# Attention before two MoE layers on one core: zero-padded q in place of stacked operands, the gate moved into the normaliser, the order of the steps rewritten

## The chip, the cores and the metric

One core of one Trainium2 chip. The time is that of one execution on the device in microseconds (us); less is better. The kernel before takes 941.54 us as the median of 3 runs (940.49 to 942.72).

## What is computed

In short form:

```python
scores = scale * np.matmul(q, k.transpose(0, 1, 3, 2))      # B, H, S, D = 4, 8, 576, 64
a = softmax(causal(scores)); local = np.matmul(a, v)
q_p = np.where(q > 0, q, np.exp(q) - 1.0) + 1.0
mem_out = (q_p @ M_prev) / (q_p @ z_prev + 1e-6)
x = g * mem_out + (1 - g) * local                            # g = sigmoid(beta), one per head
h = x @ w_in; solu = h * softmax(h)                          # 2304 tokens, 512 -> 1024
x = (layernorm(solu) * g_ln) @ w_out                         # -> 512
out = (sigmoid(x @ w_gate) * (x @ w_val)) @ w_out2           # 512 -> 1536 -> 512
```

Weights of the MoE layers arrive as 64-bit floats and are turned into 32-bit ones on the chip.

## The kernel before

The attention works on 16 pairs of heads (4 batches by 4 pairs). The two heads of a pair lie on partitions 0 to 63 and 64 to 127. For a pair n the steps are: q and k are loaded and transposed on PE (`tq_p`, `tk_p`), scaled and split into a high part in the fast matmul format and a rest (`tq_h`, `tq_l` at L270 and L274; `tk_h`, `tk_l`); the scores are computed in five blocks (`s0_p` to `s4_p`, L366 to L389: block i is 128 queries against 128(i+1) keys for both heads, block 4 the last 64 queries of both heads against all 576 keys); DVE adds the mask, copies the block to SBUF and takes its maximum (`s_m`, L409), ACT takes the exponential and the row sum (`s_e`, L417), POOL multiplies by the reciprocal of the sum (`n_p`, L426); PE transposes the blocks (`g`, `t`, `tt`, `tc`), DVE or ACT copies them out of PSUM, and PE multiplies by v (`x_a`, L496) on top of the memory part (`x_m`, L481).

A score needs three products: high q with high k, low q with high k, high q with the rest of k. From pair 1 on, the kernel before does the first two as one matmul: Z (L286) holds the high and the low part of one head of q stacked on 128 partitions, W (L313) the high part of k twice. Z, W and Zm (high q with the other head's half zeroed, for the third product) are filled by ten transfers from SBUF to SBUF for each pair (`tq_d`, `tk_d`, L293, L296, L316). Block 4 uses qb, a block-diagonal copy of the last queries that POOL writes (`tq_b`, L279). In pair 0 the three products are matmuls over 64 partitions (L385).

The gate g is applied to the memory matrix by POOL (`sm`, L363). One sixteenth of w_in is converted for each pair (`cv_d` load; `cv_a`, `cv_b` on DVE, L105, L106, L114, L115; `cv_r` on ACT, L109; `cv_p`, four operations on POOL, L529, L530, L135, L138).

The table ORDER sets the order of the work by hand: a loop walks it once for each value of `it` from -3 to 18, and an entry such as `tq_p:1` issues that step for pair it+1. Each engine runs its own share of that order strictly one after another. PSUM is divided among three tags: `s`, two buffers of two banks each, which the transposes of q, k and E and the five score blocks take in turn; `t`, two buffers, for the transposed blocks; `x`, two buffers. A step that takes a buffer waits until the buffer's user before last has been copied out.

After the attention come the first MoE layer (`Moe1`) and the second (`Moe2`), whose code the change does not touch.

Of the kernel before, what the change touches and what calls it, by code (L numbers as in the profile page):

```python
# [8 lines left out]
F32 = mybir.dt.float32  # L9
# [11 lines left out]
ORDER = """  # L21
s4_e:-1 s1_p:0 tf_c:-1 cv_a:-1 ph_e:0 s1_m:0 tq_p:1 g1_p:-1 a14:-2 a12:-2 tq_b:0 n2_p:-1 a13:-2 g1_c:-1 tq_h:1
a10:-2 a01:-2 a00:-2 n3_p:-1 s0_p:0 tq_l:1 n4_r:-1 g0_p:-1 t1_p:-1 s2_p:0 cv_r:-1 s1_e:0 g0_c:-1 ph_m:0 n4_p:-1
t1_c:-1 s0_m:0 tk_d:1 cv_b:-1 lv:-1 x1_c:-2 tt_p:-1 x0_c:-2 tt_c:-1 ph_g:0 t3_p:-1 lk:2 s2_m:0 t3_c:-1 s3_p:0
s0_e:0 s4_p:0 lq:2 sm:-1 cv_p:-1 t2_p:-1 tc_p:-1 x0_m:-1 s2_e:0 ph_r:0 tq_d:1 t2_c:-1 cv_d:0 ph_s:0 s3_m:0 lz:2
n01_r:0 s3_e:0 tk_p:2 x1_m:-1 tc_c:-1 s4_m:0 tk_h:2 n23_r:0 a11:-1 t0_p:-1 tf_p:0 t0_c:-1 n1_p:0 n0_p:0 tk_l:2
""".split()
# [20 lines left out]
def kernel(  # L48
# [16 lines left out]
    nc = tc.nc  # L65
# [42 lines left out]
    def f64_r(ex):  # L108
        nc.scalar.activation(ex, ex, AF.Relu, bias=ebias, scale=16.0)  # L109

    def f64_b(raw, ex, mt):
        top = raw[:, :, 1]
        low = raw.rearrange("p n t -> p (n t)").bitcast(U16).rearrange("p (n u) -> p n u", u=4)[:, :, 1]
        nc.vector.scalar_tensor_tensor(ex, top, -0x80000000, ex, ALU.bitwise_and, ALU.bitwise_or)  # L114
        nc.vector.scalar_tensor_tensor(f32(mt), low, 2.0**-16, mt, ALU.mult, ALU.add)  # L115

# [27 lines left out]
    class Attention:  # L144
        def __init__(self, sb, ps, xe):
# [152 lines left out]

# [7 lines left out]
        def tk_l(self, n, r):  # L306
            r["kl"] = self.sb.tile([P, S], F32R, tag="kl", name=f"kl{n}", bufs=2)
            nc.vector.tensor_sub(r["kl"], r["kps"], f32(r["kh"]))

        def tk_d(self, n, r):  # L310
            if n == 0:
                return
            W = self.sb.tile([P, 2, S0], F32R, tag="W", name=f"W{n}", bufs=2)  # L313
            for hh in range(2):
                for d in range(2):
                    nc.sync.dma_start(  # L316
                        f32(W[64 * d : 64 * d + 64, hh]), f32(r["kh"][64 * hh : 64 * hh + 64, :S0])
                    )
            r["W"] = W

# [39 lines left out]

        def sm(self, n, r):
            hp = pairs[n][1]
            nc.gpsimd.tensor_scalar(r["mt"], r["mt"], self.gp[:, hp : hp + 1], 1.0, ALU.mult, ALU.mult)  # L363


        def s_p(self, n, r, i):  # L366
            ps = r["s", i] = self.psum([P, 2, 512], f"sc{n}_{i}")
            kh, kl = r["kh"], r["kl"]
            if i == NB:
                qb = self.qb[n % 2]  # L370
                for j in range(2):
                    x = ps[:, j, : S // 2]
                    sl = slice(j * S // 2, (j + 1) * S // 2)
                    nc.tensor.matmul(x, qb[:, 0], kh[:, sl], start=True, stop=False)
                    nc.tensor.matmul(x, qb[:, 1], kh[:, sl], start=False, stop=False)
                    nc.tensor.matmul(x, qb[:, 0], kl[:, sl], start=False, stop=True)
                return
            w = P * (i + 1)
            for hh in range(2):
                sl = slice(64 * hh, 64 * hh + 64)  # L380
                x = ps[:, hh, :w]
                if n == 0:
                    F = r["F"]
                    for j, (c, kk) in enumerate(((1, kh), (0, kh), (0, kl))):
                        nc.tensor.matmul(x, F[sl, c, w - P : w], kk[sl, :w], start=j == 0, stop=j == 2)  # L385
# [495 lines left out]
```

## Time and profile before

| | |
|---|---|
| median of 3 runs | 941.54 us |
| the profiled execution, its own time | 940.15 us |
| its span in the profile | 938.4 us |
| attention, to the first matmul of `h` | 263.83 us |
| the two MoE layers | 674.57 us |
| granted TensorE clock, mean | 0.993 |

The profile is of one execution. PE is the matmul engine, PEld its weight load, DVE, ACT and POOL the vector, scalar and GpSimd engines, SP the engine that issues the transfers. A row of the timeline gives a start, a duration and, in brackets, how long the engine stood idle before it and which instruction's end released it. Durations of neighbouring rows overlap a little, since an engine starts the next instruction before the last one's result is written; where the text counts what an instruction adds to a queue it takes the distance from start to start. The end of a matmul is modelled: a matmul's 0.4 us include the way of its last column through the array, while the next one may start 0.12 to 0.23 us after it.

### The profile page before, as it was taken

The numbers are of one execution on the slowest core, as the hardware profiler recorded it, in microseconds if no ns is written. First come the engines' busy times: TensorE is split into PE (matmuls) and PEld (weight loads), VectorE is DVE, ScalarE is ACT, GpSimd is POOL, SyncE is SP. The second block draws the span as 40 slices with busy tenths as digits, with TensorE's granted clock in tenths as the row PEclk, the third lists the DMA queues.
The fourth block names the chain that finished last, engine by engine and source line by source line (L and its number), as shares of the span: only waits on it lengthen the run. The fifth ranks groups of instructions, "written<-read, shape, count | busy, mean of one in ns | idle before, by whom it ended". The sixth has DMA issues, their size and how long they took to land.

```text
span 938.4 us, 13939 instructions
## 1 busy us (share of the span) xinstructions
PE 881.5 (94%) x5104; PEld 732.5 (78%) x5104; DVE 572.7 (61%) x1268; ACT 415.0 (44%) x877; POOL 315.3 (34%) x420
## 2 busy tenths in 40 slices
PE   5888888888899999999999999999999999999998
PEld 3656665656677899999989888888888888888887
DVE  5788888888769564584764237637338845333324
ACT  3677777777757655565545233212112212111111
POOL 3777777778956321120510014112005203000000
PEclk9899999999999999999999999999999999999999
DMA  6776777777422110030220003203002200000112
GB/s 137 162 178 155 169 174 163 170 163 165 111 64 72 46 46 24 23 90 1 70 67 1 1 1 113 67 1 90 1 1 91 90 0 1 1 1 1 45 45 112
DMA packets 88291, 68.28 MB, mean 73 GB/s; under 512 B 65056, under 2 KB 65056, under 8 KB 88224
## 3 DMA queue, kind: packets, MB, share of 16 engines
q1 hardware_dynamic: 88224, 67.41, 27.9%
q8 instruction: 40, 0.66, 0.3%
q14 instruction: 27, 0.22, 0.1%
HBM read 43.00 MB, written 4.72 MB: 51 GB/s over the span
## 4 chain that ended last, share of the span: by engine, by line
PE 65%; DVE 5%; POOL 3%; issue 1%; ACT 1%; DMA 0%; POOLq 0%; ACTq 0%; DVEq 0%
PE gv L759 32%; PE po L778 16%; PE po L677 9%; PE h L626 7%; PE pl L665 1%; POOL p L426 1%; DVE exwo L106 0%; DVE exwo L115 0%; DVE exwo L105 0%; DMA rawg<-in_moe_w_gate_dram 0%; DVE exwo L114 0%; DVE lnT L132 0%; POOL rd L646 0%; PE x L496 0%; DVE hm L633 0%
## 5 line engine op out<-in xcount | busy, mean ns | idle before, releaser
L765 DVE TENSOR_TENSOR sg<-sg,gv 128x512 f32<-128x512 f32 (+1 forms) x60 | 38.0, 633 | 175.9 <-ACT sg L764 175.9
L764 ACT ACTIVATE sg<-gv 128x512 f32<-128x512 f32 (+1 forms) x60 | 33.1, 552 | 233.7 <-PE gv L759 233.7
L759 PE MATMUL gv<-xx,gh 128*128 128x512 f32 (+1 forms) x480 | 136.2, 368 | 0.2 <-ACT xx L131 0.2
L759 PE MATMUL gv<-xx,vh 128*128 128x512 f32 (+1 forms) x480 | 136.1, 368 | 0.0
L677 PE MATMUL po<-lnT,woh 128*128 128x256 f32 x576 | 105.5, 285 | 1.0 <-ACT woh L604 0.7
L759 PEld LDWEIGHTS gv<-xx,gh 128*128 128x128 f32 x480 | 87.3, 188 | 16.1 <-issue 0.4
L759 PEld LDWEIGHTS gv<-xx,vh 128*128 128x128 f32 x480 | 87.1, 189 | 15.0
L426 POOL TENSOR_SCALAR p<-p,rs 128x256 f32<-128x256 f32 (+2 forms) x144 | 83.9, 598 | 32.0 <-DVE rs L422 26.1
L677 PEld LDWEIGHTS po<-lnT,woh 128*128 128x128 f32 x576 | 91.0, 193 | 2.5 <-ACT woh L604 0.9
L759 PE MATMUL gv<-xx,gl 128*128 128x512 f32 (+1 forms) x240 | 88.3, 368 | 0.0
L759 PE MATMUL gv<-xx,vl 128*128 128x512 f32 (+1 forms) x240 | 88.3, 368 | 0.0
L417 ACT ACTIVATE p<-p,nm 128x256 f32<-128x256 f32 (+2 forms) x144 | 83.0, 581 | 8.1 <-DVE nm L409 8.0
L626 PE MATMUL h<-wih,xs 128*128 128x512 f32 x288 | 81.8, 397 | 2.6 <-DVE e L639 2.5
L778 PE MATMUL po<-oh,GVxs 128*128 128x512 f32 x216 | 84.1, 389 | 0.0
L778 PE MATMUL po<-ol,GVxs 128*128 128x512 f32 x216 | 84.1, 389 | 0.0
L778 PE MATMUL po<-oh,GVe 128*128 128x512 f32 x216 | 84.0, 389 | 0.0
L677 PE MATMUL po<-lnT,wol 128*128 128x256 f32 x288 | 81.9, 286 | 1.1 <-POOL wol L138 1.1
L785 DVE TENSOR_TENSOR X<-X,po 128x512 f32<-128x512 f32 x90 | 61.4, 684 | 23.2 <-PE po L778 23.2
L135 POOL TENSOR_SCALAR gh<-exg 128x512 fp32r<-128x512 f32 x12 | 9.8, 826 | 173.2 <-PE gv L759 142.1
L626 PEld LDWEIGHTS h<-wih,xs 128*128 128x128 f32 x288 | 53.5, 190 | 13.9 <-ACT e L648 2.9
L409 DVE CUSTOM_DVE_ANT_0 p<-sc,mask 128x256 f32<-128x256 f32 (+3 forms) x128 | 56.1, 474 | 2.1 <-PE sc L389 2.1
L677 PEld LDWEIGHTS po<-lnT,wol 128*128 128x128 f32 x288 | 55.4, 193 | 1.3 <-POOL wol L138 1.3
(363 smaller groups left out, 1855.5 us busy)
## 6 DMA issues: line engine op xcount, KB each, us to landing
W<-kh SPq DMA_DIRECT2D x60, 128.0 KB, 3.1
Z<-F SPq DMA_DIRECT2D x60, 128.0 KB, 2.4
rawg<-in_moe_w_gate_dram SPq DMA_DIRECT2D x12, 512.0 KB, 3.9
rawv<-in_moe_w_val_dram SPq DMA_DIRECT2D x12, 512.0 KB, 3.9
rawo<-in_moe_w_out_dram SPq DMA_DIRECT2D x12, 512.0 KB, 3.4
out_dram<-X SPq DMA_DIRECT2D x18, 256.0 KB, 2.0
kt<-in_k_dram SPq DMA_DIRECT2D x32, 128.0 KB, 2.6
qt<-in_q_dram SPq DMA_DIRECT2D x32, 128.0 KB, 2.7
```

Of the source, the lines that this page charges most:

```text
L135: nc.gpsimd.tensor_scalar(hi, src, scale, 1.0, ALU.mult, ALU.mult)
L409: nc.vector.tensor_tensor_reduce(p, x, m, -1.0, 3.0e38, ALU.add, ALU.min, nm)
L417: nc.scalar.activation(p, p, AF.Exp, bias=nm, scale=-1.0, accum_out=r["sum"][:, c : c + 1])
L426: nc.gpsimd.tensor_scalar(p, p, r["rs"][:, c : c + 1], 1.0, ALU.mult, ALU.mult)
L626: nc.tensor.matmul(ph[:, j * 512 : j * 512 + 512], xs[:, s, c], w[:, j * 512 : j * 512 + 512], start=(c == 0 and s == 0 and w is hi), stop ...
L665: nc.tensor.transpose(pl[:, c], ln[:, f * P : f * P + P], ident)
L677: nc.tensor.matmul(po[:, :GW], w[:, m * P : m * P + P], L[:, x, c], start=(c == 0 and n == 0), stop=(c == NF1 - 1 and n == 2),)
L759: nc.tensor.matmul(ps[:, j, :w], wt[:, c, fs], xx[:, x, c], start=(c == 0 and n == 0), stop=(c == NC - 1 and n == 2),)
L764: nc.scalar.activation(sg[:, :w], ps[:, 0, :w], AF.Sigmoid)
L765: nc.vector.tensor_mul(sg[:, :w], sg[:, :w], ps[:, 1, :w])
L778: nc.tensor.matmul(po, GV[x][:, f, sl], wt[:, f], start=(f == 0 and n == 0), stop=(f == NCH - 1 and n == 2),)
L785: nc.vector.tensor_add(acc[:, t], acc[:, t], po)
```

## The change

- `tq_h` and `tq_l` write straight from PSUM into q2, one tile for each parity of the pair, zeroed once at the start: 128 partitions by (high, low) by 1152 columns. Head 0's 576 columns have zeros on partitions 64 to 127, head 1's have zeros on partitions 0 to 63, and the last 64 queries of the two heads lie side by side, so that block 4 is a slice of it. That takes three instructions on ACT and three on DVE (64 partitions by 576, 512 and 64 columns) in place of one each over 128 by 576.
- All five score blocks are three matmuls over 128 partitions for each half, in all pairs, against kh and kl. Z, W, Zm, F and qb go, with `tq_d`, `tk_d`, `tq_b`.
- `sm` goes. The row normaliser takes the gate: the 128x10 addition on DVE becomes a scalar_tensor_tensor with a second tile g10 (1 + exp(-beta) five times over, built once in `gates`).
- Of the four POOL operations of the w_in conversion one stays (`cv_p`); the scaling goes to ACT (in `cv_r`), the high part to ACT (`cv_h`), the rest to DVE (`cv_l`), and the scaling by 2^-20 also enters `cv_b`'s constant. The raw tile gets two buffers.
- ORDER is new.

```diff
 ORDER = """
-s4_e:-1 s1_p:0 tf_c:-1 cv_a:-1 ph_e:0 s1_m:0 tq_p:1 g1_p:-1 a14:-2 a12:-2 tq_b:0 n2_p:-1 a13:-2 g1_c:-1 tq_h:1
...
+n23_r:-1 s1_e:0 s4_m:0 tt_c:-1 tc_c:-1 s3_m:0 lk:1 cv_r:-1 n3_p:-1 s0_e:0 s4_e:0 x1_c:-2 a00:-2 g1_p:-1 tf_p:0
...
+CVL = "v"
...
-    def f64_b(raw, ex, mt):
+    def f64_b(raw, ex, mt, scale=None):
...
+            nc.vector.scalar_tensor_tensor(f32(mt), low, 2.0**-16 * scale, f32(mt), ALU.mult, ALU.add)
...
-            self.F1 = sb.tile([P, 2, S], F32R, tag="tmp", name="F1")
...
-                qb = sb.tile([P, 2, P], F32R, tag=f"qb{n}", name=f"qb{n}")
-                nc.gpsimd.memset(f32(qb), 0.0)
-                self.qb.append(qb)
-                Zm = xe.tile([P, 2, S0], F32R, tag="e", name=f"Zm{n}")
+
+                q2 = sb.tile([P, 2, 2 * S], F32R, tag=f"q2{n}", name=f"q2{n}")
                 for hh in range(2):
-                    nc.gpsimd.memset(f32(Zm[64 - 64 * hh : 128 - 64 * hh, hh]), 0.0)
-                self.Zm.append(Zm)
+                    nc.gpsimd.memset(f32(q2[64 - 64 * hh : 128 - 64 * hh, :, hh * S : hh * S + S]), 0.0)
+                self.q2.append(q2)
...
+        def q_parts(self, n, r):
+
+            for hh, src, dst in ((0, 0, 0), (1, 0, S + TL), (1, S0, S)):
+                sl, w = slice(64 * hh, 64 * hh + 64), S if hh == 0 else S0 if src == 0 else TL
+                yield r["qps"][sl, src : src + w], *(self.q2[n % 2][sl, c, dst : dst + w] for c in range(2))
+
         def tq_h(self, n, r):
...
+            for x, hi, _ in self.q_parts(n, r):
+                nc.scalar.mul(hi, x, QS)
 
         def tq_l(self, n, r):
...
+            for x, hi, lo in self.q_parts(n, r):
+                nc.vector.scalar_tensor_tensor(lo, x, QS, f32(hi), ALU.mult, ALU.subtract)
...
-        def tq_b(self, n, r):
...
-        def tq_d(self, n, r):
...
-        def tk_d(self, n, r):
...
-            nc.vector.tensor_scalar_add(nr, nr, 1e-6)
+            nc.vector.scalar_tensor_tensor(nr, nr, 1e-6, self.g10[:, pairs[n][1]], ALU.add, ALU.mult)
...
-        def sm(self, n, r):
-            hp = pairs[n][1]
-            nc.gpsimd.tensor_scalar(r["mt"], r["mt"], self.gp[:, hp : hp + 1], 1.0, ALU.mult, ALU.mult)
...
+            q2, kh, kl = self.q2[n % 2], r["kh"], r["kl"]
+            for j in range(2):
+                if i == NB:
+
+                    ks, x = slice(j * S // 2, (j + 1) * S // 2), ps[:, j, : S // 2]
+                    qs = [q2[:, c, S0 : S0 + P] for c in range(2)]
                 else:
...
+                    w = P * (i + 1)
+                    ks, x = slice(0, w), ps[:, j, :w]
+                    q0 = w - P + j * (S + TL)
+                    qs = [q2[:, c, q0 : q0 + P] for c in range(2)]
+                for m, (c, kk) in enumerate(((0, kh), (1, kh), (0, kl))):
+                    nc.tensor.matmul(x, qs[c], kk[:, ks], start=m == 0, stop=m == 2)
...
-            r["raw"] = self.sb.tile([P, 256, 2], I32, tag="raw", name=f"raw{n}")
+            r["raw"] = self.sb.tile([P, 256, 2], I32, tag="raw", name=f"raw{n}", bufs=2)
...
         def cv_r(self, n, r):
             f64_r(r["ex"][:, 0])
+            nc.scalar.mul(f32(r["ex"][:, 1]), r["ex"][:, 1], 2.0**-20)
...
-            nc.gpsimd.tensor_scalar(m, m, 2.0**-20, 1.0, ALU.mult, ALU.mult)
-            nc.gpsimd.tensor_mul(m, m, e)
-            hi, lo = (x[:, 256 * j : 256 * j + 256] for x in wi[c])
-            pool_hi(hi, m)
-            pool_lo(lo, m, hi)
+            m, _, _ = self.cv_parts(n, r)
+            nc.gpsimd.tensor_mul(m, m, f32(r["ex"][:, 0]))
+
+        def cv_h(self, n, r):
+            m, hi, _ = self.cv_parts(n, r)
+            nc.scalar.copy(hi, m)
+
+        def cv_l(self, n, r):
+            m, hi, lo = self.cv_parts(n, r)
+            (nc.vector if CVL == "v" else nc.gpsimd).tensor_sub(lo, m, f32(hi))
```

PE around `trf`, the transpose of E that the first `trq` after it waits for through its copy. Names carry the pair: trf5 is pair 5's, sc6_1 block 1 of pair 6's scores, t5a1 and t5b0 transposed blocks. Before:

```order
L258 MATMUL trf5_1388<-ident_58,E5_1195 128x128 x5
L388 MATMUL sc6_1_1402<-W6_1272,Z6_1344 128x256
L389 MATMUL sc6_1_1402<-kl6_1182,Zm0_120 128x256
L388 MATMUL sc6_1_1402<-W6_1272,Z6_1344 128x256
L389 MATMUL sc6_1_1402<-kl6_1182,Zm0_120 128x256
L258 MATMUL trq7_1419<-ident_58,qt1_94 128x128 x5
```

and now (x4_0 is a product with v of pair 4; between the two pieces stand the rest of t5b2 and two rows of t5b0):

```order
L352 MATMUL sc6_3_1432<-kl6_1356,q20_117 128x512
L459 MATMUL x4_0_1345<-A4_1271,vt1_106 64x256 x2
L398 MATMUL t5a1_1472<-ident_58,p5_1_1193 128x128 x2
L265 MATMUL trf6_1475<-ident_58,E6_1298 128x128 x5
L411 MATMUL t5b3_1481<-ident_58,p5_3_1241 128x128 x2
L352 MATMUL sc6_2_1492<-kh6_1343,q20_117 128x384 x2
L352 MATMUL sc6_2_1492<-kl6_1356,q20_117 128x384
L352 MATMUL sc6_2_1492<-kh6_1343,q20_117 128x384 x2
L352 MATMUL sc6_2_1492<-kl6_1356,q20_117 128x384
...
L411 MATMUL t5b0_1504<-ident_58,p5_2_1329 128x128
L411 MATMUL t5b0_1504<-ident_58,p5_3_1241 128x128
L265 MATMUL trq7_1518<-ident_58,qt1_93 128x128 x5
```

Before, one score block of four matmuls stands between `trf` and the next `trq`; now a transposed block, score block 2 with six matmuls, and three more transposed blocks (t5b3, t5b2, t5b0) stand there. Block 2 now follows `trf`, and block 3 stands before it.

DVE around the low part of q (F before, q20 now; kl is k's low part, nr the normaliser, nm a block's maximum). Before:

```order
L409 ISA nm_1417 128x1
L128 COPY A5_1438<-t5a1_1425 128x2x128
L274 SCALAR_TENSOR_TENSOR F7_1440<-trq7_1419,F7_1440 128x576
L421 SCALAR_TENSOR_TENSOR rs5_1258<-sum5_1257,o9_273 128x1
L422 RECIPROCAL rs5_1258<-rs5_1258 128x1
L330 TENSOR_SCALAR E6_1412<-E6_1412 128x640
L331 SCALAR_TENSOR_TENSOR E6_1412<-qt0_93,E6_1412 128x640
```

and now:

```order
L306 TENSOR_SCALAR E6_1298<-E6_1298 128x640
L307 SCALAR_TENSOR_TENSOR E6_1298<-qt0_92,E6_1298 128x640
L284 SCALAR_TENSOR_TENSOR q20_117<-trq6_1305,q20_117 64x576
L284 SCALAR_TENSOR_TENSOR q20_117<-trq6_1305,q20_117 64x512
L284 SCALAR_TENSOR_TENSOR q20_117<-trq6_1305,q20_117 64x64
L295 TENSOR_TENSOR kl6_1356<-trk6_1337,kh6_1343 128x576
L321 TENSOR_REDUCE nr6_1378<-G6_1358 128x10
L322 SCALAR_TENSOR_TENSOR nr6_1378<-nr6_1378,g10_174 128x10
L323 RECIPROCAL nr6_1378<-nr6_1378 128x10
L372 ISA p6_1_1406,nm_1407<-sc6_1_1392,mask_94 128x256
```

Before, the low part of q stands behind a copy of a transposed block (A5) and ahead of the E and block 0 of pair 6; now E stands ahead of it, and it is followed by k's low part and the normaliser before the first score block (pair 6, block 1) is read.

## Rows read from the trace of the kernel before

**Rows 1.** The page, part 1: busy time of each engine, share, instructions.
```profile
PE 881.5 (94%) x5104; PEld 732.5 (78%) x5104; DVE 572.7 (61%) x1268; ACT 415.0 (44%) x877; POOL 315.3 (34%) x420
```

**Rows 2.** Windows view, four stretches: start:end us, length, busy us per engine, PEclk, DMA, GB/s.
```profile
0.00:25.33 25.33, 13.55 (x60) 9.49 (x60) 14.44 (x58) 10.57 (x27) 9.99 (x25) 0.98 0.67 140
25.33:239.82 214.49, 179.97 (x1344) 133.02 (x1344) 181.87 (x529) 159.34 (x418) 163.22 (x252) 0.99 0.73 167
239.82:263.83 24.01, 21.98 (x175) 14.83 (x174) 13.80 (x47) 15.99 (x41) 19.45 (x31) 1.00 0.24 70
263.83:938.40 674.57, 665.98 (x3530) 575.20 (x3528) 362.57 (x635) 229.12 (x393) 122.67 (x114) 0.99 0.13 40
```

**Rows 3.** Timeline of PE, one pair: start us, us, line, out<-in, [idle before <-releaser].
```profile
118.82 0.28 PE L388 MATMUL sc<-W,Z 128*128 128x256 f32 x1
118.94 0.28 PE L389 MATMUL sc<-kl,Zm 128*128 128x256 f32 x1
120.17 0.77 PE L258 MATMUL trq<-ident,qt 128*128 128x128 f32 x5 [0.95 <-ACT f L128]
...
123.68 0.28 PE L388 MATMUL sc<-W,Z 128*128 128x128 f32 x1
123.79 0.27 PE L389 MATMUL sc<-kl,Zm 128*128 128x128 f32 x1
...
125.15 0.33 PE L388 MATMUL sc<-W,Z 128*128 128x384 f32 x1
125.32 0.34 PE L389 MATMUL sc<-kl,Zm 128*128 128x384 f32 x1
...
126.62 0.39 PE L388 MATMUL sc<-W,Z 128*128 128x512 f32 x1
126.85 0.40 PE L389 MATMUL sc<-kl,Zm 128*128 128x512 f32 x1
128.08 0.40 PE L374 MATMUL sc<-kh,qb 128*128 128x288 f32 x1 [0.84 <-DVE nm L409]
...
129.62 0.65 PE L481 MATMUL x<-f,mt 128*64 128x256 f32 x4
131.01 0.77 PE L258 MATMUL trk<-ident,kt 128*128 128x128 f32 x5 [0.74 <-DVE nm L409]
```

**Rows 4.** Timeline of ACT in the same pair.
```profile
126.61 0.38 ACT L128 COPY Bt<-t6b 128x256 f32<-128x256 f32 x1
...
133.62 0.58 ACT L128 COPY Bt<-t6b 128x512 f32<-128x512 f32 x1 [1.18 <-PE t6b L448]
...
134.88 0.63 ACT L128 COPY f<-trf 128x576 f32<-128x576 f32 x1
...
136.49 0.65 ACT L270 ACTIVATE F<-trq 128x576 fp32r<-128x576 f32 x1 [0.34 <-DMA W<-kh]
```

**Rows 5.** Timeline of DVE in the same pair.
```profile
121.78 0.76 DVE L274 SCALAR_TENSOR_TENSOR F<-trq,F 128x576 fp32r<-128x576 f32 x1 [0.17 <-ACT F L270]
...
130.25 0.09 DVE L409 DVE_READ_ACCUMULATOR2_ANT nm<- 128x1 f32 x1
...
130.87 0.09 DVE L409 DVE_READ_ACCUMULATOR2_ANT nm<- 128x1 f32 x1
...
135.63 0.29 DVE L105 TENSOR_SCALAR ex<-raw 128x256 int32<-128x256 int32 x1 [2.23 <-DMA raw<-in_moe_w_in_dram]
...
137.17 0.76 DVE L274 SCALAR_TENSOR_TENSOR F<-trq,F 128x576 fp32r<-128x576 f32 x1
```

**Rows 6.** Source views of L114, L115, L346: count, duration ns min/median/max.
```profile
L114 DVE SCALAR_TENSOR_TENSOR ex<-raw,ex x16: 422/1586/1598, 31.5 to 254.3; 128x256 int32<-128x256 int32 x16
...
L115 DVE SCALAR_TENSOR_TENSOR ex<-raw,ex x16: 409/412/1779, 33.0 to 254.9; 128x256 f32<-128x256 uint16 x16
...
L346 DVE TENSOR_SCALAR nr<-nr x16: 173/741/748, 21.3 to 248.5; 128x10 f32<-128x10 f32 x16
```

**Rows 7.** The page, part 6: the transfers into W.
```profile
W<-kh SPq DMA_DIRECT2D x60, 128.0 KB, 3.1
```

More of the change, by code (lines that the diff above doesn't have):

```diff
@@ L21 @@
 ORDER = """
-s4_e:-1 s1_p:0 tf_c:-1 cv_a:-1 ph_e:0 s1_m:0 tq_p:1 g1_p:-1 a14:-2 a12:-2 tq_b:0 n2_p:-1 a13:-2 g1_c:-1 tq_h:1
[L23 to L26, printed above, removed]
+n23_r:-1 s1_e:0 s4_m:0 tt_c:-1 tc_c:-1 s3_m:0 lk:1 cv_r:-1 n3_p:-1 s0_e:0 s4_e:0 x1_c:-2 a00:-2 g1_p:-1 tf_p:0
+t3_p:-1 g1_c:-1 tf_c:0 n2_p:-1 t3_c:-1 x0_c:-2 s2_p:0 t2_p:-1 t0_p:-1 cv_b:-1 ph_e:1 t2_c:-1 n4_r:0 n01_r:0 tq_p:1
+cv_p:-1 n1_p:0 lz:1 t0_c:-1 t1_p:-1 g0_p:-1 cv_h:-1 tq_h:1 s2_m:0 t1_c:-1 ph_m:1 tk_p:1 tk_h:1 x0_m:-1 x1_m:-1
+a13:-1 tq_l:1 tk_l:1 ph_g:1 n0_p:0 n4_p:0 cv_d:1 lv:0 a12:-1 a11:-1 a14:-1 a10:-1 ph_r:1 lq:2 ph_s:1 s3_e:0 s2_e:0
+a01:-1 s1_p:1 s0_p:1 s1_m:1 tt_p:0 s0_m:1 g0_c:-1 tc_p:0 s4_p:1 cv_l:-1 s3_p:1 cv_a:0
 """.split()
 COPY = dict(tf="s", tc="v", tt="s", kh="s", x0="v", x1="s", g0="s", g1="v", t0="s", t1="s", t2="s", t3="s")
+CVL = "v"
 def f32(ap):
@@ L114, in f64_b @@
         nc.vector.scalar_tensor_tensor(ex, top, -0x80000000, ex, ALU.bitwise_and, ALU.bitwise_or)
-        nc.vector.scalar_tensor_tensor(f32(mt), low, 2.0**-16, mt, ALU.mult, ALU.add)
+        if scale is None:
+            nc.vector.scalar_tensor_tensor(f32(mt), low, 2.0**-16, mt, ALU.mult, ALU.add)
+        else:
+            nc.vector.scalar_tensor_tensor(f32(mt), low, 2.0**-16 * scale, f32(mt), ALU.mult, ALU.add)
     def load_f64(raw, ex, mt, src):
@@ L170, in __init__ @@
                 nc.vector.memset(t[64:128, tail], 0.0)
-            self.p4, self.qb, self.Zm = [], [], []
+            self.p4, self.q2 = [], []
             for n in range(2):
@@ L194, in gates @@
             sb, bt = self.sb, self.bt
-            nc.vector.tensor_scalar_add(bt, bt, 1.0)
+            nc.vector.tensor_scalar(bt, bt, 1.0, 1e30, ALU.add, ALU.min)
+            bth = bt.rearrange("p (a h) -> p a h", h=2)
+            self.g10 = sb.tile([P, HP, 10], F32, tag="g10", name="g10")
+            for c in range(NB + 1):
+                nc.vector.tensor_copy(self.g10[:, :, 2 * c : 2 * c + 2], bth)
             nc.vector.reciprocal(bt, bt)
-            bth = bt.rearrange("p (a h) -> p a h", h=2)
             self.gp = sb.tile([P, HP], F32, tag="gp", name="gp")
@@ L308, in tk_l @@
             nc.vector.tensor_sub(r["kl"], r["kps"], f32(r["kh"]))
-        def tk_d(self, n, r):
[L311 to L319, printed above, removed]
         def ph_e(self, n, r):
@@ L359, in tf_c @@
             copy("tf", r["f"], r["fps"])
-        def sm(self, n, r):
-            hp = pairs[n][1]
-            nc.gpsimd.tensor_scalar(r["mt"], r["mt"], self.gp[:, hp : hp + 1], 1.0, ALU.mult, ALU.mult)
         def s_p(self, n, r, i):
             ps = r["s", i] = self.psum([P, 2, 512], f"sc{n}_{i}")
[L368 to L385, printed above, removed]
-                else:
-                    Z, W = r["Z"], r["W"]
-                    nc.tensor.matmul(x, Z[:, hh, w - P : w], W[:, hh, :w], start=True, stop=False)
-                    nc.tensor.matmul(x, self.Zm[n % 2][:, hh, w - P : w], kl[:, :w], start=False, stop=True)
+            q2, kh, kl = self.q2[n % 2], r["kh"], r["kl"]
[3 more added lines that the diff above has]
+                    qs = [q2[:, c, S0 : S0 + P] for c in range(2)]
+                else:
+                    w = P * (i + 1)
[4 more added lines that the diff above has]
+                    nc.tensor.matmul(x, qs[c], kk[:, ks], start=m == 0, stop=m == 2)
         def parts(self, r, i):
@@ L521, in cv_r, with cv_parts @@
             f64_r(r["ex"][:, 0])
+            nc.scalar.mul(f32(r["ex"][:, 1]), r["ex"][:, 1], 2.0**-20)
         def cv_b(self, n, r):
-            f64_b(r["raw"], r["ex"][:, 0], r["ex"][:, 1])
+            f64_b(r["raw"], r["ex"][:, 0], r["ex"][:, 1], 2.0**-20)
+        def cv_parts(self, n, r):
+            c, j = divmod(n, 4)
+            return f32(r["ex"][:, 1]), *(x[:, 256 * j : 256 * j + 256] for x in wi[c])
         def cv_p(self, n, r):
-            c, j = divmod(n, 4)
-            m, e = f32(r["ex"][:, 1]), f32(r["ex"][:, 0])
-            nc.gpsimd.tensor_scalar(m, m, 2.0**-20, 1.0, ALU.mult, ALU.mult)
-            nc.gpsimd.tensor_mul(m, m, e)
-            hi, lo = (x[:, 256 * j : 256 * j + 256] for x in wi[c])
-            pool_hi(hi, m)
-            pool_lo(lo, m, hi)
+            m, _, _ = self.cv_parts(n, r)
[6 more added lines that the diff above has]
+            (nc.vector if CVL == "v" else nc.gpsimd).tensor_sub(lo, m, f32(hi))
         def run(self):
```

26 lines of the change are left out of this document (removed).

## The prediction

> **What bounds the kernel now.** The page's first part puts PE at 94% of the span [rows 1], which reads as if only PE's work counted. The windows view says where that is false. I cut the span at the first score block of pair 1, that of pair 15 and the first matmul of `h` [rows 2]. The last stretch, 674.57 us of MoE with PE busy for 665.98, is left alone by the change. In the middle stretch, 214.49 us for 14 pairs or 15.32 us each, nobody is full: per pair PE is busy for 12.86, DVE 12.99, ACT 11.38, POOL 11.66.
>
> So a ring of waits sets the pace there, and PE's timeline shows it. In one pair PE stands idle three times, for 0.95, 0.84 and 0.74 us, before `trq`, score block 4 and `trk` [rows 3]. All three wait for one of the two `s` buffers in PSUM. Counted from start to start they are longer, since a matmul's modelled end lies behind the moment at which the next may start: the last of 512 columns starts at 126.85 and takes 0.23, so block 4, at 128.08, came 1.00 late; `trq` came 1.11 late (118.94 + 0.12 to 120.17); for `trk` I take its 0.74 and the same 0.17 more, 0.91. That is 3.0 us of waits and 12.3 us of PE's own work in a pair.
>
> The ring itself: DVE runs through from the low part of q (121.78) to the maximum of block 3 (130.95), 9.2 us; that frees `trk` at 131.01; PE goes on to a transposed block that ACT copies at 133.62; ACT's copy of f (134.88 to 135.51) frees the next `trq`, which is `trq` at 120.17 a pair later; ACT's high part follows at 136.49 and DVE's low part at 137.17 [rows 3 to 5]. 121.78 to 137.17 is 15.39 us: the ring is closed, and it passes through DVE, PE and ACT.
>
> **The change part by part.** *Transfers out.* Ten of 128 KB a pair, 60 into W alone [rows 7]. Their only mark on the ring is 0.34 us before ACT's high part [rows 4]. DVE's wait of 2.23 us for raw [rows 5] ends in time: the low part of q starts at 137.17, and ACT's high part, which it needs, ends at 136.49 + 0.65 = 137.14 [rows 4]. So neither raw's second buffer nor the freed queue is worth anything by itself. If the ring stayed, 0.34 us a pair, 5 us in all, is what the transfers could give.
>
> *Scores.* Each head's block gets a third matmul: 8 more a pair. Start to start one costs 0.11 us at 128 columns, 0.12 at 256, 0.17 at 384 and 0.23 at 512 [rows 3], so 2 x 0.63 = 1.26 us a pair. The zeros save nothing: a matmul's cost is its columns. PE's own work goes from 12.3 to 13.6; by its busy time, which counts the overlaps, from 12.86 to 14.1. These are the bounds of a pair if PE is the bound.
>
> *Split q.* ACT's 0.65 and DVE's 0.76 [rows 4, 5] are for 576 columns; half the partitions save nothing, so 576 + 512 + 64 columns cost twice that: ACT +0.65, DVE +0.76.
>
> *w_in.* POOL loses three operations here, and `sm` and `tq_b`; it was not on the ring, which I count at nothing. ACT gains two copies of 256 columns, 0.38 each [rows 4]; DVE gains a subtraction of 256 columns, between 0.41 (L115 at its median) and 1.78 (its longest) [rows 6]; I take 0.41.
>
> *Gate in the normaliser.* The 10-element addition takes 0.74 but 0.17 at its shortest [rows 6]. It becomes a scalar_tensor_tensor; between no gain and 0.57 of gain; I take none.
>
> Sum by engine per pair: PE 13.6 to 14.1, DVE 12.99 + 0.76 + 0.41 = 14.2, ACT 11.38 + 0.65 + 0.76 = 12.8, POOL below 11.7. DVE's 14.2 holds stalls: L114 takes 1.59 in nearly every pair and 0.42 at its shortest [rows 6]. It now runs on other neighbours; without that stall DVE needs 13.0. So if no ring closes above them, PE is the bound.
>
> *The order.* Does one close? What counts is how much PE work stands between a user of an `s` buffer and the user after next. Before, four matmuls (block 1, 0.5 us) stood between `trf` and `trq`, while ACT had a copy and an exponential to do before f. Now t5b3, score block 2 with six matmuls of 384 columns (6 x 0.17) and three transposed blocks stand there, over 2 us, and f's copy is 0.63 [rows 4]. `trk` now waits for block 2's maximum, with three transposed blocks and `trq` between. The tightest is block 2, which waits for block 3's: DVE needs 0.63 + 0.69 there [rows 5], against two products, two transposed blocks and `trf` on PE. In all three the cover is at least about the wait; what can be late is DVE, which has two conversion steps and two normalisers ahead of block 2's maximum. I therefore take PE as the bound, with a quarter of a microsecond of waits left: 13.9 us a pair, between 13.6 and 14.1.
>
> *Sum.* Middle stretch: 14 x 13.9 = 194.6 in place of 214.5, -19.9. Start: pair 0 loads q first and computes its first score block within the start-up pass, but now waits for its normaliser and the larger gate set-up before its first maximum; bounds -4 and +3 of 25.33, I take -1. End: 24.01 us with PE busy for 21.98 [rows 2]; pair 15's last blocks still go through ACT, POOL, PE in turn, but one pass deeper in the loop; bounds -4 and +2, I take -2. Together -22.9. The profiled execution took 940.15, so 917.3; the median of the runs, 941.54, lies 1.4 above it: 918.6, and I write **918.5**. With a pair at 13.6 and the better ends it is 909; at 14.1 and the worse ends 929.
>
> **The rivals.** *DVE becomes the bound.* Its operations with two SBUF operands (the conversion's two, E, the normalisers, the new subtraction) stand still while POOL works: L114 shows 0.42 and 1.59, L115 0.41 and once 1.78 [rows 6]. If the new order puts both conversion steps behind POOL instructions, DVE needs 14.2 + 1.4 = 15.6 at worst and about 14.7 with one more short stall. For: DVE gains most. Against: POOL loses five instructions a pair, so there is less to stand behind. At 14.7 a pair: 14 x 0.62 = 8.7 and 3 at the ends, **930**. The Trainium skill's page "SBUF — State Buffer", under "Who interferes with whom", gives the reason: such a DVE instruction and a GpSimd one that reads SBUF share a port pair, and the later one is blocked for the whole of the other. By that rule `cv_l` on DVE is one more candidate for being blocked, up to a whole POOL instruction. The trace agrees in L114's two durations.
>
> *The waits move to block 2's maximum, and it is slower.* On DVE, `cv_b`, `n4_r` and `n01_r` stand ahead of it; `n4_r` waits for ACT's exponential of block 4, which is fifth in ACT's queue, and ACT is now loaded with 12.8. If that runs late, `trk` and all PE work behind it wait. With waits as long as the three of today, 2.5 us by their brackets [rows 3], a pair takes 13.6 + 2.5 = 16.1: 14 x 0.8 = +11 and -3 at the ends, **950**. It decides from 1.7 us on (15.3 - 13.6). For: PE's added work is certain, the cover is not. Against: ACT has a microsecond of slack.
>
> *Nothing moves.* The ring of DVE, PE and ACT re-forms at the old length, the transfers having been hidden and the matmuls filling idle time: **941**. For: it has DVE's longer q step in it. Against: the steps around `trq` and `trk` are the ones reordered.
>
> **How the numbers follow.** PE the bound, 909 to 924: 0.58. DVE or a mild stall, 924 to 937: 0.25. Nothing, 937 to 944: 0.05, and slower, up to 955: 0.12. The range 911 to 934 leaves out some 2 in 10, most of it on the slow side. Under 0.2% (1.9 us) a measurement of this kernel can't tell from no change. Faster 0.84, same 0.04, slower 0.12.
>
> **What would show it.** Right: pairs 13.6 to 14.1 us apart; PE without idle time over 0.3 us in the middle stretch; no wait for raw; the MoE part still at 674 to 676. The first rival shows as DVE rows of 1 us and more in E, `cv_b` or `cv_l`, and PE waiting for maxima; the second as one long wait of `trk` for a maximum, and DVE before it for ACT. Wrong altogether: a pair above 15.3, or an MoE stretch that changes by more than 2 us.

## The result, and the profile after

The changed kernel takes 915.03 us (median of 4 runs, 913.95 to 916.32), the one before 941.01 in the same runs (940.02 to 942.72): a ratio of 0.9723, 95% interval 0.9703 to 0.9742. The prediction said 918.5, between 911 and 934. The profiled execution took 914.82, with a span of 913.0.

The page's first part after, to be read against [rows 1]: PE's share rises from 94% to 97%, POOL loses 48 us.

```profile
PE 888.3 (97%) x5224; PEld 753.2 (82%) x5224; DVE 567.2 (62%) x1321; ACT 432.1 (47%) x941; POOL 267.0 (29%) x322
```

The windows view, cut at the same instructions as [rows 2] (start:end, length, busy us of PE, PEld, DVE, ACT, POOL, PEclk, DMA share, GB/s):

```profile
0.00:27.75 27.75, 14.49 (x56) 11.84 (x56) 17.15 (x68) 11.10 (x26) 12.87 (x20) 0.94 0.48 105
27.75:216.43 188.68, 187.75 (x1481) 152.72 (x1481) 175.34 (x574) 175.52 (x480) 119.73 (x172) 0.99 0.40 92
216.43:238.38 21.95, 20.80 (x163) 14.77 (x161) 12.65 (x46) 16.36 (x45) 11.79 (x18) 1.00 0.15 52
238.38:913.00 674.62, 665.21 (x3530) 573.85 (x3528) 362.10 (x635) 229.08 (x393) 122.57 (x114) 1.00 0.13 40
```

Stretch by stretch: start +2.42 us (forecast -1), middle -25.81 (forecast -19.9), end -2.06 (forecast -2), MoE +0.05 (forecast 0). In the middle PE is now busy for 187.75 of 188.68 us. The first pair of that stretch is longer than the rest (from 27.75 to 43.02, 15.3 us, with the granted clock at 0.50 of full speed, the 1.2 GHz level, from 29.0 to 32.4); after it a pair takes 13.29.

One such pair on PE's timeline, against [rows 3]. Each half of a score block now takes two matmuls with high k (one row, x2) and one with low k:

```profile
96.15 0.50 PE L352 MATMUL sc<-kh,q 128*128 128x256 f32 x2
96.49 0.28 PE L352 MATMUL sc<-kl,q 128*128 128x256 f32 x1
96.61 0.40 PE L352 MATMUL sc<-kh,q 128*128 128x256 f32 x2
...
96.96 0.33 PE L352 MATMUL sc<-kh,q 128*128 128x128 f32 x2
...
98.95 0.63 PE L352 MATMUL sc<-kh,q 128*128 128x512 f32 x2
99.42 0.40 PE L352 MATMUL sc<-kl,q 128*128 128x512 f32 x1
99.65 0.63 PE L352 MATMUL sc<-kh,q 128*128 128x512 f32 x2
...
103.98 0.71 PE L265 MATMUL trq<-ident,qt 128*128 128x128 f32 x5
...
105.40 0.71 PE L265 MATMUL trk<-ident,kt 128*128 128x128 f32 x5
...
109.44 0.50 PE L352 MATMUL sc<-kh,q 128*128 128x256 f32 x2
```

No row of the pair has an idle bracket. The waits view of PE from 45 to 216 us (who waited for whom: us, times, longest) says the same for the whole loop; before it had three entries, the three of the ring:

```profile
PE sc L374 <- DVE nm L409: 10.6, 11, 1.6
PE trq L258 <- ACT f L128: 10.5, 11, 1.0
PE trk L258 <- DVE nm L409: 7.6, 11, 0.7
```

After, there is one wait left:

```profile
PE sc L352 <- DVE nm L372: 0.3, 1, 0.3
```

DVE's stalls of [rows 6] are gone: in the source views (duration in ns, min/median/max) both steps of `cv_b` are at their short length in all 16 pairs (the first is shown, the second takes 414/417/419), and so is the normaliser's small operation, now a scalar_tensor_tensor.

```profile
L117 DVE SCALAR_TENSOR_TENSOR ex<-raw,ex x16: 412/414/417, 35.8 to 232.3; 128x256 int32<-128x256 int32 x16
```
```profile
L322 DVE SCALAR_TENSOR_TENSOR nr<-nr,g x16: 169/170/171, 13.9 to 216.6; 128x10 f32<-128x10 f32 x16
```

And this is why the start became longer. DVE's timeline at 20 us: the scaling of the MoE's small vector `gl` stands ahead of block 3's maximum, and its load, last of the start's loads, lands at 20.17. PE then waits 1.94 us for that maximum.

```profile
20.19 0.17 DVE L795 TENSOR_SCALAR gl<-gl 128x8 f32<-128x8 f32 x1 [2.56 <-DMA gl<-in_moe_g_ln_dram]
20.27 0.68 DVE L372 CUSTOM_DVE_ANT_0 p<-sc,mask 128x512 f32<-128x512 f32 x1
```

### The profile page after: what moved, and what is told of

It reads as the page before. It is cut to its first block, busy times and chain, and to the rows that moved or that the text cites. A ratio compares the mean times of both kernels' runs of the same rounds, so it can differ in the third digit from the quotient of the medians.

```text
span 913.0 us, 13960 instructions
## 1 busy us (share of the span) xinstructions
PE 888.3 (97%) x5224; PEld 753.2 (82%) x5224; DVE 567.2 (62%) x1321; ACT 432.1 (47%) x941; POOL 267.0 (29%) x322
## 4 chain that ended last, share of the span: by engine, by line
PE 87%; DVE 7%; POOL 2%; ACT 1%; issue 1%; DMA 1%; SPq 1%; DVEq 0%; POOLq 0%; ACTq 0%
PE gv L730 32%; PE po L749 16%; PE po L648 9%; PE sc L352 8%; PE h L597 7%; PE x L459 5%; PE x L444 2%; PE pl L636 1%; PE trq L265 1%; DVE p L372 1%; PE trk L265 1%; PE trf L265 1%; DVE exwo L109 1%; DVE exwo L108 0%; DVE exwo L119 0%
## 5 line engine op out<-in xcount | busy, mean ns | idle before, releaser
L389 POOL TENSOR_SCALAR p<-p,rs 128x256 f32<-128x256 f32 (+2 forms) x144 | 78.3, 561 | 36.4 <-ACT ex L112 16.4
L352 PE MATMUL sc<-kh,q 128*128 128x256 f32 (+4 forms) x320 | 79.5, 340 | 9.0 <-DVE nm L372 5.4
L352 PEld LDWEIGHTS sc<-kh,q 128*128 128x128 f32 x320 | 54.2, 200 | 14.6 <-DVE nm L372 6.5
```

The lines of the kernel that those rows point to most:

```text
L352: nc.tensor.matmul(x, qs[c], kk[:, ks], start=m == 0, stop=m == 2)
L389: nc.gpsimd.tensor_scalar(p, p, r["rs"][:, c : c + 1], 1.0, ALU.mult, ALU.mult)
```

## The experiments

Two theories stood against each other first. **Theory:** the new order opened the ring, so PE's work became the bound, in spite of 120 more matmuls. **Rival:** the gain comes from the transfers and POOL operations taken out, and the order only follows.

**1. The change in the order of before.** ORDER is that of before without `tq_b`, `tq_d`, `tk_d`, `sm`, which have no work any more:

```
- n23_r:-1 s1_e:0 s4_m:0 tt_c:-1 tc_c:-1 s3_m:0 lk:1 ...
+ s4_e:-1 s1_p:0 tf_c:-1 cv_a:-1 ph_e:0 s1_m:0 tq_p:1 ...
+ ... cv_p:-1 cv_h:-1 cv_l:-1 t2_p:-1 tc_p:-1 x0_m:-1 ...
```

> The changed kernel with the order of before (less the four dropped steps, cv_h and cv_l put behind cv_p). If the new order made the gain, the ring of DVE, PE and ACT closes again: 15.4 us a pair, less 0.34 of the wait for W, plus 0.65 on ACT and 0.76 on DVE, so 15.4 to 16.5 a pair and 940 to 958 us, with waits before trq, block 4 and trk. If the dropped transfers and POOL work made it, the pair stays at 13.3 to 13.7 and the time at 915 to 921.

Measured: 962.99 us (962.25 to 963.68), 1.0256 times before (1.0231 to 1.0282). Slower than before, and above both ranges. PE's timeline shows the three waits of [rows 3] with the same releasers, and a pair of 16.92 us (the next `trq` starts at 131.47):

```profile
114.55 0.78 PE L261 MATMUL trq<-ident,qt 128*128 128x128 f32 x5 [0.70 <-ACT f L131]
...
124.02 0.53 PE L348 MATMUL sc<-kh,q 128*128 128x288 f32 x2 [1.24 <-DVE nm L368]
...
126.85 0.78 PE L261 MATMUL trk<-ident,kt 128*128 128x128 f32 x5 [0.61 <-DVE nm L368]
```

The length can be worked out. The ring of before took 15.39 us and runs through ACT's high part of q and DVE's low part. Both are now three instructions, and ACT and DVE rows say what they take:

```profile
115.36 1.36 ACT L276 ACTIVATE q<-trq 64x576 fp32r<-64x576 f32 x3 [0.23 <-PE trq L261]
```
```profile
116.76 1.60 DVE L280 SCALAR_TENSOR_TENSOR q<-trq,q 64x576 fp32r<-64x576 f32 x3 [0.74 <-ACT q L276]
```

15.39 + (1.36 - 0.65) + (1.60 - 0.76) = 16.94 with the 0.65 and 0.76 of [rows 4, 5], and 16.92 was measured. Leg by leg it fits too: from the low part's start to the end of block 3's maximum it takes 10.03 us (116.76 to 126.79; before 9.18), from ACT's high part to DVE's low part 1.39 (132.29 to 133.68; before 0.68), and the rest 5.50 (before 5.53). So without the order the change lengthens the ring by its own q split; what the transfers gave back is not to be seen.

**2. The operands of before in the new order.** F, Z, W, Zm, qb, their transfers and matmuls as before, at the places where the new order has their sources (cut to the main lines):

```
+ tk_h:1 tk_d:1 ... tq_l:1 tq_d:1 tq_b:1
-     for m, (c, kk) in enumerate(((0, kh), (1, kh), (0, kl))):
+     nc.tensor.matmul(x, Z[:, hh, w - P : w], W[:, hh, :w], start=True, stop=False)
+     nc.tensor.matmul(x, self.Zm[n % 2][:, hh, w - P : w], kl[:, :w], start=False, stop=True)
```

> The changed kernel with the operands of before (F, Z, W, Zm, qb and their transfers, two matmuls a head) in the new order. If the new order needs operands that are there at once, the first score block waits for the transfers: q's low part now ends 1.3 us before it, while four and two transfers take 2.5 and 1.2 us to issue and 2.4 to land, so 3 to 6 us more a pair, 16 to 19 us, 950 to 1000 us. If transfers are hidden in this order too, PE has 1.1 us less than now and DVE's 12.7 bounds the pair: 905 to 909.

Measured: 1001.44 us (1001.07 and 1001.81), ratio 1.0669 (1.0635 to 1.0702), a little above the upper end of what was expected. PE's waits from 60 to 250 us, and the windows view of one pair of 19.52 us:

```profile
PE sc L396 <- DMA Z<-F: 30.0, 10, 3.3
PE sc L397 <- DMA Zm<-F: 15.4, 10, 1.7
```
```profile
117.76:137.28 19.52, 15.04 (x100) 11.97 (x99) 12.14 (x40) 11.89 (x33) 8.95 (x15) 0.83 0.58 129
```

4.5 us a pair are waits for the transfers, and after the first of them the granted clock is down: in this pair at 0.50 from 126.9 to 133.7, 0.83 as the mean of the pair. The new order transposes q 5.5 us ahead of the first score block that uses it (103.98 and 109.44 in the changed kernel), where the old one had 13.7 (120.17 to 133.89); a transfer's 3.1 us [rows 7], behind the split and nine others, do not fit in there. So the two parts, as they are written here, need each other: the new order with the old operands loses 63 us, the old order with the new scores 25 (before took 938.13 in these runs), together they gain 26 (from 941.01). Another place for the transfers in the new order was not tried, and no run splits the new order into its moves.

**3 and 4. Is PE the bound?** Two ways to take PE work off. In *half_rows* blocks 0 to 3 use 64 rows for each head, so that the zeros are not multiplied:

```
+ rows = slice(64 * j, 64 * j + 64)
- qs = [q2[:, c, q0 : q0 + P] for c in range(2)]
+ qs = [q2[rows, c, q0 : q0 + P] for c in range(2)]
+ ko = kk[:, ks] if i == NB else kk[rows, ks]
```

> The changed kernel with blocks 0 to 3 as matmuls over each head's own 64 partitions of q2, kh and kl, without the zero rows; same products. If a matmul costs its columns whatever its rows, nothing changes: 915. If two matmuls on different halves of the array run at once, as pair 0 of the kernel before suggests (its matmuls of 512 columns over 64 partitions started two at a time), PE loses 1.5 to 2 us a pair and DVE, idle for some 0.57 of 13.29, bounds it at 12.7: 14 x 0.57 = 8 less, 905 to 909.

In *two_products* the product of low q and high k is left out:

```
- enumerate(((0, kh), (1, kh), (0, kl)))
+ enumerate(((0, kh), (0, kl)))
```

> The changed kernel without the product of low q with high k in all score blocks (left out, so scores are less exact). If PE is the bound, its 1.1 us a pair go until DVE at 12.7 bounds it: 905 to 909. If DVE or ACT already set the pace, 914 to 916.

Measured: 906.13 us (904.97 to 906.5; ratio 0.9651, 0.963 to 0.9672) and 903.68 (902.83 and 904.52; 0.9627, 0.9595 to 0.9659). Both are faster than the change, and its pair of 13.29 us becomes 12.80 and 12.79, so its loop was bound by PE's work. (Part of the gain stands ahead of the loop: pair 1 starts at 26.59 and 24.67 in place of 27.75. In *two_products* the scaling of gl stands later in DVE's queue, behind block 3's maximum, as in experiment 7.) Both end at nearly the same pair, although they take off different work; the windows view shows a pair of *half_rows*:

```profile
104.85:117.65 12.80, 12.55 (x109) 9.12 (x107) 12.51 (x42) 12.37 (x35) 8.38 (x13) 1.00 0.46 114
```

In both, DVE's waits view from 45 to 214 us is empty, where the changed kernel has one entry, the slack that DVE still had:

```profile
DVE p L372 <- PE sc L352: 7.0, 24, 0.4
```

So at 12.8 us DVE is the next bound: in *half_rows* the chain that ended last runs from 100 to 140 us through DVE's rows alone. In *two_products* it goes half through DVE and half through PE, so there the two are level. No run shows a gain from taking work off DVE; experiments 8 and 10 tried. The rows of block 3 in *half_rows* are the surprise told of at the end.

**5. The late load of gl.**

```
- nc.sync.dma_start(gl, moe_g_ln.rearrange("(c p) -> p c", p=P))
- nc.vector.tensor_scalar_mul(gl, gl, 2.0**-20)
+ if it == 1: nc.sync.dma_start(gl, ...)
+ if it == 3: nc.vector.tensor_scalar_mul(gl, gl, 2.0**-20)
```

> The change, with the load of moe_g_ln and its scaling taken out of the start: loaded in pass 1 of the loop, scaled in pass 3. Theory of the start: in the changed kernel DVE stood behind that scaling for 2.56 us (its load was issued at 17.60, behind vt, qt and kt, and landed at 20.17) with the first maximum queued behind it, so the first block of pair 1 comes some 2 us earlier: 912.5 to 913.5 us, all of it before pair 1, the loop at 13.28 us a pair as before. Rival: pair 0 waits for its normaliser, the gates and q's low part anyway: 914.5 to 915.5 us, and the wait for gl only turns into another one.

Measured: 914.14 us (913.64 to 914.65), ratio 0.9719 (0.9706 to 0.9733), which the interval of the change (0.9703 to 0.9742) does not tell apart. By the trace the theory is right on its place and wrong on the sum: pair 1's first block starts at 25.68, 2.07 us earlier, but the first matmul of `h` only 0.83 us earlier (237.55). The rest is lost to the clock. A window of this kernel from the start of pair 1 (PEclk, the granted clock as a share of 2.4 GHz, is the third number from the end):

```profile
25.68:32.30 6.62, 6.62 (x26) 6.19 (x27) 4.66 (x19) 4.54 (x17) 4.76 (x8) 0.50 0.00 0
```

and three of the changed kernel, where pair 1 starts at 27.75:

```profile
22.20:25.50 3.30, 3.23 (x14) 2.73 (x13) 1.92 (x6) 0.88 (x2) 0.94 (x2) 0.50 0.00 0
25.60:28.90 3.30, 1.16 (x7) 0.76 (x6) 3.11 (x6) 3.27 (x10) 2.96 (x4) 1.00 0.00 0
29.00:32.30 3.30, 3.30 (x18) 3.30 (x17) 2.30 (x15) 2.31 (x9) 1.72 (x2) 0.50 0.00 0
```

Before pair 1 PE stands still for 2.1 us (for q's low part) in the late load, for 1.9 in the changed kernel. In the late load the clock falls to the 1.2 GHz level at 25.5, just before pair 1, and 6.6 us of the pair run at it. In the changed kernel one such stretch lies ahead of the pause and only 3.4 us lie in pair 1. Both are back at 2.4 GHz at much the same time, 32.3 and 32.4 us, and pair 1 takes 16.42 us in the late load (25.68 to 42.10) and 15.27 in the changed kernel. The clock is also in the 2.07 us themselves: block 3's maximum comes 1.27 us earlier (19.00 against 20.27), and most of the other 0.8 is PE work that the changed kernel does at the lower level before the pause (block 2's six matmuls take 1.68 us against 1.16).

**6. w_in's last steps back on POOL.** `cv_h` and `cv_l` leave ORDER, and `cv_b` its constant (not shown).

```
- nc.scalar.mul(f32(r["ex"][:, 1]), r["ex"][:, 1], 2.0**-20)
...
+ nc.gpsimd.tensor_scalar(m, m, 2.0**-20, 1.0, ALU.mult, ALU.mult)
  nc.gpsimd.tensor_mul(m, m, f32(r["ex"][:, 0]))
+ pool_hi(hi, m)
+ pool_lo(lo, m, hi)
...
```

> The change, with w_in's last steps put back on POOL as four operations in a row (scale, product, high part, low part), none on ACT and DVE. Theory (PE is the bound of the loop, DVE and ACT have some slack): POOL's three more operations, about 2.1 us a pair, fall into its idle time of over 4 us a pair; 914 to 916.5 us. Rival (DVE's operations with two SBUF operands stand still while POOL works, and DVE's slack is only 0.57 us a pair): two or three more short stalls make DVE the bound, 13.6 to 14.5 us a pair, 919 to 932 us, with DVE rows of about 1 us in the conversion steps, E or the normalisers.

Measured: 914.53 us (913.74 to 916.06), ratio 0.9726 (0.9712 to 0.9739): no difference, and a pair is 13.29 us as in the change. The stalls that the rival named do come, but DVE has room for them. E's second step and the normaliser's small operation, 0.82 and 0.17 in the change, on DVE's timeline here, and what is left of DVE's idle time (7.0 us in the change):

```profile
106.60 1.23 DVE L307 SCALAR_TENSOR_TENSOR E<-qt,E 128x640 f32<-128x640 f32 x1
...
111.05 0.55 DVE L322 SCALAR_TENSOR_TENSOR nr<-nr,g 128x10 f32<-128x10 f32 x1
```
```profile
DVE p L372 <- PE sc L352: 3.3, 12, 0.4
```

With PE as the bound, spreading w_in's steps is worth nothing that these runs can tell.

**7. The gate back on M.** `sm` is back in ORDER and g10 is not built (not shown).

```
- nc.vector.scalar_tensor_tensor(nr, nr, 1e-6, self.g10[:, pairs[n][1]], ALU.add, ALU.mult)
+ nc.vector.tensor_scalar_add(nr, nr, 1e-6)
+ nc.gpsimd.tensor_scalar(r["mt"], r["mt"], self.gp[:, hp : hp + 1], 1.0, ALU.mult, ALU.mult)
```

> The change, with the gate put back on M (one POOL operation a pair on the memory tile, none in the normaliser, no g10 to set up). Theory (PE is the bound, the gate only moves 0.2 to 0.6 us of side work): the loop stays at 13.28 us a pair; the start is up to 1 us shorter, as five copies and their place ahead of the first maximum go: 914 to 915.5 us. Rival (the gate's move was worth something in the loop: the POOL operation blocks DVE again, or delays f's user x): over 917 us, with a pair above 13.45 us.

Measured: 912.93 us (912.25 to 913.61), ratio 0.9707 (0.9693 to 0.972), which the interval of the change does not tell apart. In the trace the loop is as in the change (13.27 us a pair), so the gate's move gained nothing there. The start is 2.3 us shorter (pair 1 at 25.48), more than was expected: besides the copies, the scaling of gl has slipped behind block 3's maximum in DVE's order, so nothing waits for its load.

```profile
18.79 0.69 DVE L373 CUSTOM_DVE_ANT_0 p<-sc,mask 128x512 f32<-128x512 f32 x1 [1.65 <-PE sc L353]
...
20.09 0.17 DVE L796 TENSOR_SCALAR gl<-gl 128x8 f32<-128x8 f32 x1
```

Experiment 5, where only gl moved, has pair 1 at 25.68, so 0.2 of the 2.3 us are left for the gate itself. Of the 2.3 us, 1.25 are left at the first matmul of `h` (237.13): the clock again, as in experiment 5.

**8. Half rows, the late gl, and w_in's low part on POOL** (`CVL = "p"`), to take work off the next bound, DVE.

> Three things together: scores of blocks 0 to 3 as matmuls of 64 rows for each head (906.1 us alone), moe_g_ln loaded late, and w_in's low part (a subtraction of 0.57 to 0.66 us a pair there) on POOL in place of DVE. With half rows alone DVE had no idle time at 12.80 us a pair and PE waited 0.2 us: DVE was the bound. Theory: with that subtraction off DVE a pair falls to 12.3 to 12.5 us, PE being the next bound: 14 x 0.3 to 0.5 = 4 to 7 us, and 2 us from the late load: 897 to 900 us. Rival: POOL's added operation blocks DVE's steps for as long as it freed: only the late load shows, 903.5 to 904.5 us.

Measured: 909.91 us (909.25 to 911.01), ratio 0.9677 (0.9664 to 0.9691): above both expectations. Its interval touches that of half rows alone (0.963 to 0.9672), but the trace is clear: the first matmul of `h` comes at 234.73 us against 229.59. A pair is back at 13.27 us, and DVE has a wait that nobody had thought of:

```profile
DVE ex L108 <- POOL wil L506: 12.4, 12, 1.2
```

`ex` has one buffer. Its last reader, the low part, used to run on DVE itself, ahead of the next conversion in the same queue; now DVE's first conversion step has to wait for POOL, where the subtraction is queued behind E's scaling.

**9 and 10. Half rows with the gate on M**, and the same with the low part on POOL and a second buffer:

```
- r["ex"] = self.sb.tile([P, 2, 256], I32, tag="ex", name=f"ex{n}")
+ r["ex"] = self.sb.tile([P, 2, 256], I32, tag="ex", name=f"ex{n}", bufs=2)
- CVL = "v"
+ CVL = "p"
```

> Half rows (906.1 us alone) and the gate back on M (2.1 us better than the change alone, all of it before pair 1). Theory: the two lie in different stretches and add up: a pair stays at 12.80 us, bound by DVE, the start loses some 2 us: 903.5 to 905 us. Rival: as with the late load of moe_g_ln alone, a start that comes earlier meets a lower granted clock in pair 1 and half or all of it is given back: 905 to 906.5 us.

> Half rows, the gate on M, w_in's low part on POOL, and a second buffer for ex. Without that buffer DVE's first conversion step waited 1.01 us a pair for POOL's low part, and a pair took 13.27 us. Theory: the wait was the buffer's; with two of them DVE needs 12.2 to 12.4 us a pair and PE is next at 12.3 to 12.5: 14 x 0.3 to 0.5 = 4 to 7 us under the kernel with half rows and the gate on M alone, 897 to 901 us. Rival: POOL's added operation blocks DVE's conversion steps for as long as it freed, or is itself late: no better than 903.5 us.

Measured: 903.04 us (902.87 to 903.1; ratio 0.9602, 0.9583 to 0.962) for the first, **the fastest kernel of this study**; 904.51 (904.35 to 905.79; 0.9617, 0.9599 to 0.9635) for the second. In the second kernel the second buffer did end the wait (DVE's waits view is empty again), but DVE's pair is 12.87 us, not 12.3: the rival was right. L109, an operation with one operand, takes longer beside POOL's subtraction (L109 from 106.19, the subtraction from 106.07 to 106.85). Its source view with the low part on DVE:

```profile
L109 DVE TENSOR_SCALAR ex<-raw x16: 274/286/294, 27.5 to 216.9; 128x256 int32<-128x256 int32 x16
```

and with it on POOL:

```profile
L109 DVE TENSOR_SCALAR ex<-raw x16: 277/821/823, 28.1 to 218.0; 128x256 int32<-128x256 int32 x16
```

That is 0.54 us lost of the 0.65 that the subtraction had cost DVE (its median in the first kernel), and L108 ahead of it loses 0.22 more (0.52 against 0.30): 0.76 in all. For the first of the two kernels the theory was right that the gains add up: pair 1 starts 2.4 us earlier than in *half_rows* (24.17 against 26.59), `h` 1.6 (227.96 against 229.59), at 12.80 us a pair. The other 0.8 us are given back between the two, as the rival said. Here too gl's scaling stands behind block 3's maximum in DVE's queue.

## Why the prediction was right, and where it was off

*What bounds the kernel.* Right, and shown from both sides: the ring before (experiment 1 finds it again, longer by just the steps that grew), PE after (experiments 3 and 4 take PE work off, and a pair falls from 13.29 to 12.8 us; the first matmul of `h` comes 8.8 and 10.1 us earlier, at 229.59 and 228.32, of which 1.2 and 3.1 are there at the start of pair 1).

*The order.* Right. The prediction argued that each of the three waits gets more PE work in front of it than it lasts, and all three are gone. The experiments add what it did not say: the order is worth some 50 us (ratio 1.0256 against 0.9723) and not 20, since without it the change would have been slower than before. "Nothing moves", 941, was mispriced for the same reason: it kept the ring at its old length, while the q split, which the prediction itself had priced at +0.65 and +0.76, lies on that ring. 963 was the figure.

*The size of the loop.* Off by 6 us, on the good side. "I take PE as the bound, with a quarter of a microsecond of waits left: 13.9 us a pair, between 13.6 and 14.1"; it is 13.29. The quarter of a microsecond of waits isn't there. The added matmuls cost 1.1 us a pair and not 1.26 (block 3 runs 1.40 against 1.01, block 2 1.13 against 0.78, block 1 0.81 against 0.56, block 0 0.62 against 0.50, start to start). The rest, 0.2, is rounding (12.3 + 1.26 + 0.25 is 13.8, not 13.9) and PE's own work of before, which comes to 13.29 - 1.11 = 12.18 and not 12.3; why it is shorter no run shows. The stretch gains less than 14 x 0.6 us, as its first pair takes 2.0 us more than the others, at the lower clock.

*DVE.* 14.2 with its stalls or 13.0 without: the second. With nothing idle its pair is 12.8. The rival in which POOL blocks DVE did not happen in this order, but for one row of 128x4 a pair (L384, 0.65 us at 103.38, 0.14 at its shortest), and experiments 6 and 10 show how near it was: three more POOL operations halve DVE's slack, and in the kernel where DVE is the bound, one POOL operation costs DVE all that it saves. The Trainium skill's page "SBUF — State Buffer", under "Who interferes with whom", also lists `tensor_scalar` among the operations that can take the port pair shared with GpSimd; the prediction had looked at two-operand steps only. L109's 0.29 and 0.82 agree with the page.

*The start.* Wrong: -1 forecast, +2.42 found. The step that failed is "Start: pair 0 loads q first ... I take -1". It looked at pair 0's own steps and not at what else stands in DVE's queue: the scaling of gl, ahead of block 3's maximum, costs 2.07 with what it does to the clock (experiment 5). The 0.35 that are left are still not -1; which of the start's other steps takes them was not tested. It lay within the bounds given, -4 to +3. What a shorter start is worth was missed as well: pair 1 begins at a lower clock, and 0.8 of 2.07 us come through to `h`, 1.25 of 2.3 in experiment 7.

*The end and the MoE.* -2.06 against -2, and +0.05 against 0.

*The parts that cost or give nothing.* W_in's spread: nothing (experiment 6), as its steps were not on the path. The gate: nothing in the loop and 0.2 us lost at the start, apart from gl's place in the queue (experiments 5 and 7), where the prediction had allowed up to 0.57 us a pair of gain. The transfers: 0.34 us a pair of the ring was allowed for them, and experiment 1 finds none of it. The second buffer of raw was not tried by itself.

## What to carry to other kernels

Look for the ring before counting busy time: where no engine is full, add up one round through every engine it touches, and see which steps of the change lie on it; here the same edits gave -26 us with an order that opens the ring and +25 without it. When a wait is gone, name the next bound before taking more work off: here DVE stood half a microsecond behind PE. And moving an operation to another engine moves its buffer's release too, and which operations it holds up there.

## What was not expected of the hardware

Matmuls of 64 rows for the two heads, one on partitions 0 to 63 and one on 64 to 127, run partly at the same time. Block 3, six matmuls of 512 columns, in *half_rows*:

```profile
107.35 0.75 PE L354 MATMUL sc<-kh,q 64*128 64x512 f32 x4
107.92 0.41 PE L354 MATMUL sc<-kl,q 64*128 64x512 f32 x2
108.27 0.65 PE L461 MATMUL x<-A,vt 128*64 128x256 f32 x4
```

They take 0.92 us from start to start where the same products with 128 rows take 1.40 (98.95 to 99.65 is one half). The prediction's "the zeros save nothing: a matmul's cost is its columns" fits the rows of 128 partitions, and overlooks that without the zeros the two heads' matmuls lie on different partitions and overlap. Pair 0 of the kernel before already did this: four matmuls of 512 columns in 1.02 us.

```profile
17.64 1.23 PE L385 MATMUL sc<-kh,F 64*128 64x512 f32 x4 [0.35 <-DVE nm L409]
18.66 0.64 PE L385 MATMUL sc<-kl,F 64*128 64x512 f32 x2
```

Matmuls come at half the loop's pace there: the six of 288 columns behind them start 0.24 us apart (19.63 to 20.59), in the loop 0.13 (128.32 to 128.45). That is the pace of the 1.2 GHz level (288 columns in 0.24 us are 1.2 a nanosecond), though the granted clock on record reads 1.00 there, so at the start this reading alone does not tell the pace. At 128 rows and that pace one matmul of 512 columns takes 0.43 us (17.48 to 17.91 in pair 0 of the changed kernel), so four would have taken 1.7. The Trainium skill's page "TensorE: Matmul & The Clock Gate", under "Part 3: Packing small matmuls — row/col tiling", says that matmuls on different row groups run concurrently; these rows agree, with a gain of 1.5 to 1.7 where two at a time could give 2.

The second finding is the clock at the start: a stretch that begins 2.07 us earlier, after a pause of 2.1 us, ran at the 1.2 GHz level until the same moment but for 0.1 us (32.3 against 32.4 us), so most of the time won was given back. Why the clock falls at 25.5 us in the one kernel and at 22.2 and 29.0 in the other, no run shows.
